# Half of three weight quarters requested from ScalarE's DMA queue instead of SyncE's

## The chip, the cores and the metric

The kernel runs on one core of a Trainium2 chip. A core has five engines, each with its own instruction stream: TensorE (PE, matrix multiply, with weight loads shown apart as PEld), VectorE (DVE), ScalarE (ACT), GpSimd (POOL) and SyncE (SP, which here only requests DMA transfers). ACT can request transfers too; a request stands in ACT's instruction stream between its computing instructions. Sixteen DMA engines carry out the transfers of all requesters. The metric is the device time of one execution in microseconds (us).

## What is computed

Inputs are q, k, v and an output gate of shape (4, 8, 768, 40) (batch, heads, time, head size), an input and a forget gate of shape (4, 8, 768), and two weight matrices, w_in (320 x 2048) and w_out (2048 x 320). The first block is an mLSTM cell, a recurrence over time for each batch and head, cut here to its core:

```python
m_new = np.maximum(f[t] + m, i[t])
f_stab, i_stab = np.exp(f[t] + m - m_new), np.exp(i[t] - m_new)
C = f_stab * C + i_stab * outer(v[t], k[t])
n = f_stab * n + i_stab * k[t]
y[t] = sigmoid(o[t]) * (C @ q[t]) / max(abs(n @ q[t]), 1)
```

Its output is reshaped to x of shape (3072, 320), 40 columns for each head, and goes through a feed-forward layer: `h = x @ w_in`, `g = max(0.01 * h, h)`, `out = g @ w_out`. The two weight matrices arrive as float64, since they are products of a float32 array and a float64 scalar; everything else is float32.

## The kernel before

**Work and its stages.** Time is cut into 6 chunks of 128 positions, and each chunk of each of the 4 batches is a step, s = 4 * chunk + batch, 24 in all. A step computes the cell for 8 heads in parallel form (scores, masks of decay, a carried state). The four steps of a chunk together make a group of 512 tokens for the feed-forward layer. The first chunk, steps 0 to 3, is written out by hand in `first_chunk` (L1184): it loads k, q, v and o of each step (`load_first`), does the scores and values, transposes the gated result into xT (`u_x`, copies on ACT, L861 and L862), and starts the first feed-forward units of group 0 (`ffs[0]`, `ffs[1]`). A unit of group 0 (`half`, in `ff_units`) is 20 matmuls of a 64-row slice of w_in against half of the group's tokens (L872), and an activation on ACT (L880, the leaky relu) that frees the two PSUM banks. From L1319 on a loop works through the feed-forward units of one group, with the cell's steps of the next chunk placed between them; from group 1 on with other products (L929, L1036).

**Weights.** w_in is taken in four quarters of 512 columns, n = 0 to 3 (`load_weights`, L238). A quarter's raw 64-bit words land in a buffer of 128 partitions: the lower 64 partitions hold 5 blocks of 64 rows for columns 0 to 255 of the quarter, and the upper 64 partitions the 5 blocks for columns 256 to 511 in another order (`SLOTS`, L74), so that the lower half (r = 0) is one request of 640 KB and the upper half (r = 1) two, of 512 and 128 KB. Quarters 1 to 3 (`WHOLE`) are loaded so; quarter 0 comes in two parts. Raw words of quarter 1 lie in `acts`, those of 2 and 3 in `raw`. `narrow_weights` (L280) then turns a half quarter into float32: two activations on ACT (L302, L303) and four instructions on DVE (L304 to L311). w_out follows in eight parts, narrowed in the same way.

**Order.** PE, DVE, ACT and POOL run their instructions in the order in which the program writes them (`manual_schedule`, L1281). SP's requests made through `Ordered` (L89) keep the program's order too. Where requests of different queues stand among each other is planned when the program is built, as is which semaphore counts a request's completion: eight of them are handed out in turn to the requests of both queues, and a request first waits until the transfer that last used its semaphore has landed.

Around the change, SP asks in this order: quarter 1 (three requests, 24.90 to 27.52 us), the gate values a of chunk 1, written to DRAM (L360), q of step 4, quarter 2 (28.99 to 31.59), k and v of step 4, the decay masks w of step 4 (from a in DRAM, spread over partitions), the output gate of step 4, quarter 3 (43.39 to 46.22), the output gate of step 5, k of step 5, a part of w_out, the masks of step 5, and so on. ACT asks for nothing between 4.8 and 156 us. Its stream at this place is: `prep_o(2)` and `prep_o(3)`, the tanh of the output gates (L583); the relu of `ffs[1]` (L880); the copies of xT for steps 2 and 3 (L861, L862), which the feed-forward unit that starts at 38.49 reads; the narrowing of quarter 1 (L302 at 38.16); then, in the loop, that of quarters 2 and 3 (from 43.65 and 58.52). On PE, `u_split` (L638) transposes k and q of step 4 at 45.33, and `u_parts` (L725, L731) reads step 5's scaled k (`vu`, made on POOL at L567 behind the masks, L537) at 69.41.

Of the kernel before, what the change touches and what calls it, by code (L numbers as in the profile page):

```python
# [18 lines left out]
def kernel(  # L19
# [26 lines left out]
    nc = tc.nc  # L46
# [54 lines left out]
    sync, by_act = queues = Ordered(nc.sync), Ordered(nc.scalar)  # L101
# [20 lines left out]
    for u in range(2):  # L122
        part = ident[ts(u, SL), ts(u, SL)]
        nc.gpsimd.affine_select(
            part, part, compare_op=ALU.not_equal, fill=1.0, base=0, pattern=[[-1, SL]], channel_multiplier=1,
# [80 lines left out]
    def run_of(r, at):  # L206

        ks = SLOTS[r][at:]
        return ks[0], next((i for i in range(1, len(ks)) if ks[i] != ks[i - 1] + 1), len(ks))
# [25 lines left out]

    WHOLE = (1, 2, 3)

    def load_weights(n, es=(0, 1)):  # L238

        m = n - QN  # L240
        if n < QN:
            dst = w_in[:, n, :]
        else:
            dst = w_out[:, 2 * m : 2 * m + 2, :].rearrange("p a d -> p (a d)")
        to = dst
        if wide:
            if n < 2:
                at = NF * GT - 2 * WC * (n + 1)
                raw = acts_l[:, at : at + 2 * WC].bitcast(U64)
            elif n < QN:  # L250
                raw = raw_t[:, WC * (n - 2) : WC * (n - 1)]
            elif m < 2:
                raw = w_out[:].rearrange("p f d -> p (f d)")[:, (2 + m) * WC : (3 + m) * WC].bitcast(U64)
            else:
                at = (4, 0, 1, 2, 3, 4)[m - 2] * HW
                raw = raw_t[:, at : at + HW]
            raws[n] = (raw, dst)
            to = raw
        if n < QN:
            src = moe_w_in[:, n * QC : (n + 1) * QC].rearrange("(k p) (r c) -> r p k c", p=DP, r=2)  # L260
            halves = to.rearrange("p (e k c) -> p e k c", e=2, k=KC)
            both = to.rearrange("p (k c) -> p k c", k=KC)
            if n in WHOLE:
                es = es[:1] if es[0] == 0 else ()
            for e in es:
                for r in range(2):
                    at = 0
                    while at < KC:
                        k0, n_k = run_of(r, at)
                        if n in WHOLE:  # L270
                            rows, part = both[DP * r : DP * (r + 1), at : at + n_k], src[r, :, k0 : k0 + n_k, :]
                        else:
                            rows, part = halves[DP * r : DP * (r + 1), e, at : at + n_k], src[r, :, k0 : k0 + n_k, ts(e, P)]
                        sync.dma_start(rows, part)
                        at += n_k
        else:
            rows = moe_w_out[2 * m * P : 2 * (m + 1) * P, :]
            sync.dma_start(to.rearrange("p (a d) -> p a d", d=Dm), rows.rearrange("(a p) d -> p a d", p=P))
# [41 lines left out]
    def gates(c):  # L320


        m0 = m0s.get(c)
        n = BH
        fc, il = (f0[:BH], i0[:BH]) if c == 0 else (fi[c][:, 0, :], fi[c][:, 1, :])
        F = wk.tile([n, P], F32, name="F", bufs=1)
        nc.vector.tensor_tensor_scan(F[:], fc, zeros[:n].to_broadcast([n, P]), 0.0, op0=ALU.add, op1=ALU.add)
        if c > 0:
            nc.vector.tensor_scalar(il, il, scalar1=m0[:], scalar2=None, op0=ALU.subtract)
        m = wk.tile([n, P], F32, name="m", bufs=1)  # L330
        nc.vector.tensor_tensor_scan(m[:], fc, il, -1e30 if c == 0 else 0.0, op0=ALU.add, op1=ALU.max)
        a = wk.tile([n, P], F32, name="a", bufs=1)
        nc.vector.tensor_tensor(a[:], F[:], m[:], op=ALU.subtract)
        bu = wk.tile([n, 3, P], F32, name="bu", bufs=1)
        nc.vector.tensor_tensor(bu[:, 0, :], il, F[:], op=ALU.subtract)
        if c + 1 < NB:
            m1 = wk.tile([BH, 1], F32, name="m0")
            if c == 0:
                nc.vector.tensor_copy(m1[:], m[:, P - 1 :])
            else:  # L340
                nc.vector.tensor_tensor(m1[:], m0[:], m[:, P - 1 :], op=ALU.add)
            m0s[c + 1] = m1
        if c > 0:
            na = wk.tile([BH, 1], F32, name="na")
            nc.vector.tensor_tensor(na[:], m[:, SL - 1 : SL], F[:, SL - 1 : SL], op=ALU.subtract)
        bus[c] = bu, a, (na if c > 0 else None)
# [71 lines left out]
    def load_first(s, i):  # L418

        d = st.setdefault(s, {})  # L420
        at = 4 * HW * 2 + s * Dm
        dst = (kn[:, s, :, :D], qn[:, s, :, :D], S_t[s][:, 1, :, :D], blocks(raw_l[:, at : at + Dm]))[i]
        d["k"], d["q"], d["va"], d["o"] = kn[:, s], qn[:, s], S_t[s][:, 1], raw_l[:, at : at + Dm]
        sync.dma_start(dst, (k, q, v, o_gate)[i][s, :, :P, :].rearrange("h p d -> p h d"))

    def natural(s, i):

        t = rb_t[s % NR][:, i]
        return t[:, : H * D].rearrange("p (h d) -> p h d", d=D)
# [26 lines left out]
    def raw_blocks(s, i, w):  # L456

        return blocks(rb_t[s % NR][:, i, QW : QW + RL])[:, :, :w]
# [121 lines left out]
    def prep_o(s):  # L580

        o = st[s]["o"] if s < B else natural(s, 2) if s < 2 * B else raw_blocks(s, 2, DB)
        nc.scalar.activation(o, o, AF.Tanh, scale=0.5)  # L583
# [169 lines left out]
    def u_values(s):  # L753
        d = st[s]
        pool, tag = (psc, "c") if s < 2 else (psf, "mm")
        pa = d["pa"] = pool.tile([P, H, D1], F32, name="pa", tag=tag)
        for h in range(H):
            for u in range(2):
                toks = ts(u, SL)
                nc.tensor.matmul(pa[toks, h, :], lhsT=d["w"][:, h, toks], rhs=d["va"][:, h, :D1], start=True, stop=True)  # L760
# [354 lines left out]
    def u_gates(c):  # L1115
        gates_T(c, bus.pop(c)[0])
# [67 lines left out]
    def first_chunk():  # L1184

        for n in range(2):
            for i in range(3):
                load_first(n, i)
        for n in range(2):
            load_first(n, 3)  # L1190
        load_weights(0, (0,))
        on_v, on_s = nc.vector.tensor_copy, nc.scalar.copy
        gates(0)
        gates_exp(0)
        load_fi(2)
        idle(3)
        ab = spread_masks()
        bu, a, _ = bus[0]
        a, left = replicate(a, bu)
        u_transpose(0, (on_v, on_v))  # L1200
        gates(1)
        spread_first(ab, a, left, 0)
        gates_T(0, bu)
        prep_vu(0)
        first_exps(ab, 0)
        u_scores(0)
        u_transpose(1, (on_s, on_s))
        prep_vu(1)
        prepare_tiles()
        u_values(0)  # L1210
        u_scores(1)
        ab = spread_masks()
        spread_first(ab, a, None, 2)
        e = next_exps(ab, 2)
        w, w1 = narrow_weights(0, 0), narrow_weights(0, 1)
        n0, n1 = narrow_weights(1, 0), narrow_weights(1, 1)
        prep_o(0)
        prep_o(1)
        gate(0)
        u_values(1)  # L1220
        load_first(2, 0)
        load_first(2, 1)
        load_weights(0, (1,))
        load_first(3, 0)
        load_first(3, 1)
        load_first(2, 2)
        load_first(3, 2)
        load_first(2, 3)
        load_first(3, 3)
        load_weights(1, (0,))  # L1230
        load_weights(1, (1,))
        run(e, 6)
        state(0)
        state(1)
        run(w, 2)
        u_x(0)
        gate(1)
        run(w, 4)
        u_x(1)
        state_copy(0)  # L1240
        state_copy(1)
        prepare_step(0)
        prepare_step(1)
        run(e, 2)
        ffs = ff_units(0)
        u_transpose(2, (on_s, on_s))
        run(e, 4)
        gates_exp(1)
        run(w1, 2)
        run(e, 4)  # L1250
        ffs[0]()
        run(w1, 2)
        prep_vu(2)
        prep_vu(3)
        u_scores(2)
        u_transpose(3, (on_v, on_s))
        run(w1, 2)
        u_gates(1)
        u_scores(3)
        prep_o(2)  # L1260
        prep_o(3)
        u_values(2)
        ffs[1]()
        gate(2)
        u_values(3)
        gate(3)
        u_x(2)
        state(2)
        u_x(3)
        state(3)  # L1270
        state_copy(2)
        run(n0, 4)
        state_copy(3)
        run(n0, 2)
        run(n1, 6)
        prepare_step(2)
        prepare_step(3)
        return ffs
# [160 lines left out]
```

## Time and profile before

| | |
|---|---|
| time, median of 3 runs | 473.57 us (472.79, 473.57, 474.94) |
| profiled execution: its own time | 473.84 us |
| profiled execution: its span, first to last instruction | 472.0 us |
| TensorE clock granted | 1.00 |
| SP's queue (q1) | 120944 packets, 51.15 MB |
| ACT's queue (q10) | 39984 packets, 7.17 MB |

How to read it: a profile line of the order in time has start (us), length, engine, line of the kernel, operation, what it writes <- what it reads, shape, count, and in brackets the idle time before it with what ended that. "SPq" and "ACTq" are DMA requests in the two engines' streams; their length is the time for which they hold the stream, which includes waiting for room. In the table by stage each row has the stage, its length, then for PE, PEld, DVE, ACT and POOL the busy time with the number of instructions, then the granted clock, the DMA engines' mean busy share and GB/s. "Landed" is the time of the last increment of a transfer's semaphore in the trace's records. A list of waits has: who <- what ended the wait: us in total, how many, the longest.

### The profile page before, as it was taken

Reading aid. Unit: us, or ns where it says so; the run is one execution under the profiler, and the core shown is the slowest. Engines: PE = TensorE matmul, PEld = TensorE weight load, DVE = VectorE, ACT = ScalarE, POOL = GpSimd, SP = SyncE. Lnnn points to the kernel's source line nnn. Section 1 sums busy time; section 2 is a strip of 40 time slices with the busy share of each in tenths; the row PEclk is TensorE's granted clock in tenths of the full one; section 3 lists DMA queues with packets and bytes.
Section 4 is the critical chain, followed back from the end, with each engine's and each line's share of the span. In section 5 each row is a group of like instructions: output and inputs, shape, how many; then the busy total and the mean of one; then the engine's idle time right before and its main releaser. Section 6 shows DMA issues by size and latency. Waiting matters only on the chain.

```text
span 472.0 us, 14167 instructions
## 1 busy us (share of the span) xinstructions
PE 463.1 (98%) x5716; PEld 416.3 (88%) x5716; DVE 336.8 (71%) x609; ACT 203.4 (43%) x497; POOL 171.7 (36%) x225
## 2 busy tenths in 40 slices
PE   9899999999999999999999999999999999999997
PEld 6677978777788999988999988999988999988997
DVE  5778688999479988867788867788847786104541
ACT  2657878755336511366311366311456311253210
POOL 4332377264335164923214923214822005300020
PEclk9999999999999999999999999999999999999999
DMA  9999998887732695865754865853875202100001
GB/s 130 169 192 187 188 205 220 206 181 145 153 110 65 159 166 112 176 153 129 171 119 106 181 130 126 198 114 79 188 151 124 74 9 81 58 0 2 8 8 42
DMA packets 160993, 59.21 MB, mean 125 GB/s; under 512 B 123808, under 2 KB 152352, under 8 KB 160928
## 3 DMA queue, kind: packets, MB, share of 16 engines
q1 hardware_dynamic: 120944, 51.15, 48.9%
q10 hardware_dynamic: 39984, 7.17, 9.4%
q8 instruction: 45, 0.74, 0.7%
q14 instruction: 20, 0.16, 0.1%
HBM read 51.58 MB, written 6.70 MB: 123 GB/s over the span
## 4 chain that ended last, share of the span: by engine, by line
PE 87%; SPq 5%; POOL 3%; issue 3%; DVE 1%; DMA 1%; ACT 0%; POOLq 0%
PE ph L1036 33%; PE po L929 33%; PE po L894 8%; SPq L95 5%; PE pT L813 3%; PE ph L872 3%; PE sd L725 3%; PE sd L731 1%; DMA raw<-in_o_gate_dram 1%; PE hN L785 1%; POOL w L537 1%; POOL y L576 1%; POOL S L701 1%; PE pa L760 0%; PE tk L638 0%
## 5 line engine op out<-in xcount | busy, mean ns | idle before, releaser
L929 PE MATMUL po<-w_out,acts 128*128 128x160 f32 x640 | 89.1, 300 | 0.0
L929 PEld LDWEIGHTS po<-w_out,acts 128*128 128x128 f32 x640 | 87.3, 190 | 0.6 <-ACT acts L1061 0.3
L1036 PE MATMUL ph<-xT,w_in 64*128 64x256 f32 x720 | 82.7, 378 | 0.0
L1036 PEld LDWEIGHTS ph<-xT,w_in 64*128 64x128 f32 x720 | 69.2, 187 | 8.6 <-issue 0.6
L1065 DVE TENSOR_TENSOR acts<-acts,ph 128x512 f32<-128x512 f32 x60 | 38.4, 683 | 40.7 <-PE ph L1036 40.6
L929 PE MATMUL po<-raw,acts 128*128 128x160 f32 x480 | 66.4, 300 | 0.0
L929 PEld LDWEIGHTS po<-raw,acts 128*128 128x128 f32 x480 | 65.4, 190 | 0.3
L537 POOL TENSOR_SCALAR_AFFINE_SELECT w<-w 64x512 f32<-64x512 f32 x40 | 34.0, 850 | 52.9 <-DMA w<-a_dr 51.7
L1069 ACT COPY acts<-ph 128x512 f32<-128x512 f32 x60 | 32.2, 588 | 48.8 <-PE ph L1036 48.8
L1061 ACT ACTIVATE acts<-acts 128x1024 f32<-128x1024 f32 x30 | 31.6, 1055 | 41.8 <-DVE acts L1065 32.4
L701 POOL TENSOR_TENSOR S<-S,f 40x336 f32<-40x336 f32 x36 | 30.6, 849 | 47.8 <-PE pT L813 32.1
L547 ACT ACTIVATE w<-w,gT 128x64 f32<-128x64 f32 x160 | 41.6, 337 | 11.7 <-DMA a_dr<-a 4.3
L742 DVE TENSOR_TENSOR qn<-w,sd 64x384 f32<-64x384 f32 (+1 forms) x80 | 33.4, 418 | 14.3 <-ACT acts L1069 8.4
L872 PE MATMUL ph<-xT,w_in 64*128 64x256 f32 x320 | 37.3, 381 | 0.9 <-issue 0.7
L894 PE MATMUL po<-w_out,acts 128*128 128x320 f32 x128 | 36.7, 437 | 0.0
L1036 PE MATMUL ph<-acts,w 64*128 64x256 f32 x320 | 36.3, 379 | 0.0
L827 POOL TENSOR_TENSOR xb<-xb,den 128x320 f32<-128x320 f32 x16 | 11.6, 727 | 67.0 <-DVE xb L824 64.7
L872 PEld LDWEIGHTS ph<-xT,w_in 64*128 64x128 f32 x320 | 31.9, 187 | 3.8 <-ACT w_out L303 0.9
L1036 PEld LDWEIGHTS ph<-acts,w 64*128 64x128 f32 x320 | 30.6, 187 | 3.6
L894 PEld LDWEIGHTS po<-w_out,acts 128*128 128x128 f32 x128 | 23.5, 190 | 9.2 <-ACT acts L880 0.3
L967 POOL TENSOR_TENSOR y<-y,raw 128x160 f32<-128x160 f32 x10 | 9.5, 950 | 59.5 <-ACT y L966 59.5
L612 DVE TENSOR_TENSOR qn<-kqT,ea 64x512 f32<-64x512 f32 x32 | 30.0, 939 | 0.8
(184 smaller groups left out, 732.2 us busy)
## 6 DMA issues: line engine op xcount, KB each, us to landing
rb<-in_k_dram SPq DMA_DIRECT2D x64, 80.0 KB
rb<-in_q_dram SPq DMA_DIRECT2D x64, 80.0 KB
rb<-in_o_gate_dram SPq DMA_DIRECT2D x64, 80.0 KB
ea<-a_dr SPq DMA_DIRECT2D x32, 128.0 KB
raw<-in_moe_w_out_dram SPq DMA_DIRECT2D x6, 640.0 KB
w<-a_dr ACTq DMA_DIRECT2D x24, 128.0 KB
x_dr<-x SPq DMA_DIRECT2D x64, 40.0 KB
xT<-x_dr SPq DMA_DIRECT2D x16, 160.0 KB
```

What stands on the lines that cost most here:

```text
L537: nc.gpsimd.affine_select(part, part, compare_op=ALU.is_ge, fill=-1e30, base=0, pattern=[[0, H], [1, SL]], channel_multiplier=-1,)
L547: yield nc.scalar.activation(w[:, h, :], w[:, h, :], AF.Exp, bias=gT[c][:, 0, bh : bh + 1], scale=1.0)
L612: nc.vector.tensor_tensor(mixed(s)[rows, 1 - r], d["kqT"][rows, 1].rearrange("p (h t) -> p h t", t=SL), d["ea"][rows], op=ALU.mult,)
L701: nc.gpsimd.tensor_tensor(new, old, g, op=ALU.mult)
L742: nc.vector.tensor_tensor(mixed(s)[toks, u, hs], w[toks, hs], bank[1 - u][to[u][hs.start], hs], op=ALU.mult,)
L872: nc.tensor.matmul(ph[r][:, cols], lhsT=w_row(r, slot, j), rhs=xT[DP * r : DP * (r + 1), slot, cols], start=(slot == 0), stop=(slot == KC ...
L894: nc.tensor.matmul(po[n][:], lhsT=acts[:, f, ts(n, P)], rhs=w_out[:, f, :], start=(f == 0), stop=(f == NF - 1),)
L929: nc.tensor.matmul(bank[:], lhsT=left[:, f, :], rhs=right[:, f, :], start=f == 0, stop=f == KH - 1)
L1036: nc.tensor.matmul(bank[r][:, e, :], lhsT=left(r)[rows, e], rhs=right(r)[rows], start=first and e == 0 and m == 0, stop=e == 1 and m == le ...
L1061: nc.scalar.activation(to, z, AF.Prelu, alpha=0.01)
L1065: nc.vector.tensor_tensor(to[:, 2 * r : 2 * r + 2], to[:, 2 * r : 2 * r + 2], bank[r], op=ALU.add)
L1069: nc.scalar.copy(to[:, 2 * r : 2 * r + 2], bank[r])
```

## The change

The requests for the upper 64 partitions of quarters 1, 2 and 3 of w_in, two for each quarter, are taken out of SP's order and made by ACT, all six in a row, right behind the tanh of step 3. The lower halves stay where they were on SP. The bytes, the destinations and the number of requests are the same. For quarter 1 the request comes later in the program than before, for quarter 2 a little earlier, for quarter 3 much earlier.

```diff
-    def load_weights(n, es=(0, 1)):
+    def load_weights(n, es=(0, 1), rs=None):
...
             if n in WHOLE:
                 es = es[:1] if es[0] == 0 else ()
             for e in es:
-                for r in range(2):
+                for r in ((0,) if n in WHOLE else (0, 1)) if rs is None else rs:
                     at = 0
                     while at < KC:
...
-                        sync.dma_start(rows, part)
+                        (sync if rs is None else nc.scalar).dma_start(rows, part)
                         at += n_k
...
         prep_o(2)
         prep_o(3)
+        for n in WHOLE:
+            load_weights(n, rs=(1,))
         u_values(2)
         ffs[1]()
```

## The prediction

> **What bounds the kernel now.** I read the page first: busy times, slices, chain.
>
> ```profile
> PE 463.1 (98%) x5716; PEld 416.3 (88%) x5716; DVE 336.8 (71%) x609; ACT 203.4 (43%) x497; POOL 171.7 (36%) x225
> ...
> PE   9899999999999999999999999999999999999997
> ...
> DMA  9999998887732695865754865853875202100001
> ...
> PE 87%; SPq 5%; POOL 3%; issue 3%; DVE 1%; DMA 1%; ACT 0%; POOLq 0%
> ```
>
> TensorE (PE) is busy 463.1 of 472.0 us, so the kernel can lose far more than it can gain: all PE idle time is 9 us. The change lies in slices 3 to 5 (24 to 56 us), where the DMA engines are full. The table by stage says how much PE idles there:
>
> ```profile
> 24.00:30.00 6.00, 4.90 (x53) 4.17 (x51) 4.14 (x7) 5.44 (x18) 2.55 (x5) 1.00 1.05 184
> 30.00:36.00 6.00, 6.00 (x107) 5.10 (x104) 4.46 (x16) 0.90 (x3) 1.54 (x5) 1.00 1.14 200
> 36.00:44.00 8.00, 7.36 (x89) 6.67 (x90) 6.43 (x15) 5.64 (x13) 0.25 (x1) 1.00 1.15 186
> 44.00:56.00 12.00, 11.29 (x156) 10.66 (x153) 10.08 (x17) 10.12 (x28) 5.87 (x7) 1.00 1.01 168
> 56.00:70.00 14.00, 12.91 (x338) 10.66 (x339) 9.59 (x17) 11.12 (x28) 8.54 (x11) 1.00 0.90 217
> ```
>
> The first count is PE's busy time, the number before the last the DMA share (1.00 and above is full), the last GB/s. PE idles 3.5 us in 24 to 70; from 70 to 126 it idles not at all. Next, ScalarE (ACT) where the six new requests go, in order of time:
>
> ```profile
> 28.61 0.83 ACT L583 ACTIVATE raw<-raw 128x320 f32<-128x320 f32 x2
> 34.32 0.66 ACT L880 ACTIVATE acts<-ph 128x256 f32<-128x256 f32 x2 [4.88 <-PE ph L872]
> 35.76 0.37 ACT L861 COPY xT<-xt 128x256 f32<-128x256 f32 x1 [0.78 <-PE xt L860]
> 36.09 0.48 ACT L862 COPY xT<-xe 128x384 f32<-128x384 f32 x1
> 37.42 0.37 ACT L861 COPY xT<-xt 128x256 f32<-128x256 f32 x1 [0.86 <-PE xt L860]
> ```
>
> The two tanhs (L583) of steps 2 and 3 end at 29.44; then ACT is idle 4.88 us, and later 0.78 and 0.86. Then SyncE (SP) in order of time, and what its queue waited for between 28 and 37 us:
>
> ```profile
> 28.99 2.60 SPq L95 DMA_DIRECT2D raw<-in_moe_w_in_dram x3
> 31.88 1.32 SPq L95 DMA_DIRECT2D kn<-in_k_dram  x1
> 34.50 1.02 SPq L95 DMA_DIRECT2D acts<-in_v_dram  x1
> 36.10 6.61 SPq L95 DMA_DIRECT2D w<-a_dr  x2
> ```
>
> ```profile
> SPq L95 <- DMA acts<-in_moe_w_in_dram: 1.5, 2, 1.2
> ```
>
> The second is the line that matters. The load of k for step 4 (31.88) and of v (34.50) write nothing that w_in touches, yet waited for pieces of w_in to land. The semaphore records say why: all DMAs, of SP and of ACT alike, share eight completion semaphores in turn, and a DMA waits until the one eight before it has landed. k of step 4 is the eighth behind the first piece of quarter 1 (landed 31.82), v the eighth behind the second (34.42). Landing is slow here: pieces asked at 24.9 to 30.3 landed 6.9 to 12.5 us later.
>
> Last, PE where it uses all this:
>
> ```profile
> 38.49 6.91 PE L872 MATMUL ph<-xT,w_in 64*128 64x256 f32 x60
> 45.33 0.25 PE L638 MATMUL tk<-ident,kn 64*40 64x64 f32 x2
> ...
> 69.41 0.23 PE L731 MATMUL sd<-S,vu 64*40 64x42 f32 x1 [0.90 <-POOL vu L567]
> ```
>
> **The change, part by part.** Its sum goes against the profiled execution, 473.84 us (span 472.0 and 1.8 around it), which is 0.27 above the median 473.57.
>
> *Six issues leave SP* (two each at 26 to 27.5, 29.6 to 31.6, 44 to 46.2 us). They are worth nothing by themselves: SP waits on landings and the DMA engines are full from 0 to 56 us, so an earlier request only queues. If the engines had room, the gain would be the waits that DMA feeds: 0.90 at 69.41 and at most 0.7 "issue" at 46.8.
>
> *Six issues join ACT.* SP's pieces of the same shape take 0.60 to 0.63 us unhindered, so six are 3.8. At the start of the kernel a DMA of ACT was issued 0.01 us behind the start of the activation before it (3.87 against 3.86), so they begin about 29.0 and end at 32.8, before the relu at 34.32. The cover is 4.88 us of idle time. If it is gone: ACT then owes relu 0.66, copies 0.81 and 0.81 before PE can start the 60 matmuls of 38.49, and 0.78 + 0.86 of idle time can close up. Released at T, ACT ends these at T + 2.28, against 38.23 now: PE is late by T - 35.95.
>
> *Bytes change places.* Quarter 3's upper piece (640 KB) is asked for at about 32 instead of 44 to 46. Its two parts took 51.64 to 55.14, 3.5 us of full engines; whatever it passes lands 3.5 us later. Without another delay that is k of step 4, landed 43.67, which PE wants at 45.33: 1.66 spare, 1.8 late. Masks of step 4 (landed 45.8) have 5 us: GpSimd ended that chain (vu) at 51.25, PE takes it from 56.4. Quarter 1's upper piece is asked 2.5 us later than now (landed 35.44); its reader is ACT at 38.16, 2.7 spare.
>
> *The semaphores in turn*, the term that decides. Each of ACT's six waits for the DMA eight before it in the planned order, and ACT's relu and copies queue behind. Counted from what SP may have asked by then: quarter 1's lower piece, a, q of step 4, quarter 2's lower piece, k of step 4 (all free to go by about 28.5 once two pieces are gone from before them); then ACT's first three; then v of step 4, which is free when VectorE has narrowed quarter 0 (30.98); then ACT's last three. Eight before the fourth is a, before the fifth q, before the sixth quarter 2's lower piece. So ACT is held until that lands. It lands at 39.49 now. Quarter 1's upper piece, 3.62 us of it (31.82 to 35.44), is no longer in SP's line: 35.9 if nothing of ACT's passes it. If ACT's first five do, they add 3.62, 3.27 (quarter 2, 39.49 to 42.76) and 2.99 (quarter 3's larger part, 51.64 to 54.63): 45.7. The nearest row for who goes first: ACT's 16 KB asked at 3.87 landed at 7.21, before SP's 160 KB asked at 3.01 (8.48), but 3.3 us after it was asked, where an empty queue took 1.7. So ACT's packets pass part of SP's: I take the middle, 40.8, and with the last issue, 0.62, T = 41.4. PE is late by 5.45. Behind it the 0.90 wait at 69.41 is gone, since masks of step 5 (landed 59.7) keep their time: the bytes ahead of them are the same. Sum: 473.84 + 5.45 - 0.90 = 478.4; against the median, 478.1. Ends of the term: T = 36.5 makes +0.55, eaten by the 0.90; T = 46.4 makes +10.4 - 0.9 = 9.5, so 483.1.
>
> The Trainium skill, "DMA: Bandwidth & Descriptors", section "Rules for kernel authors", says not to bother with two transfers to disjoint partition halves, since both spread over the same 16 engines and serialize. By that alone the time would stay at 473.6; it speaks against a gain and agrees with the full DMA share above, but says nothing of a held ScalarE.
>
> **Rivals.**
> 1. *ACT is not held.* The planned order puts the six early enough that the DMAs eight before them have landed (up to the o gates of step 3, landed 28.84, and quarter 1's lower piece, 31.8). For it: six fit in the idle time; SP's real order at 29 us is only just past k of step 4. Then only k of step 4 is late, 1.8 us at 45.33, of which 0.90 comes back at 69.41: 474.5 (473.2 to 475.9). This is not slower by what can be measured. It decides if ACT is released before 35.95.
> 2. *ACT is held longer.* Its 2 KB packets alternate one for one with SP's, whose q of step 4 has 160-byte packets, so all of ACT's five go first: the upper end, 483.1 (480.5 to 484.5). The same comes if the six are planned behind v of step 4, waiting for k (43.67 now). Against it: the 7.21 landing above.
> The Trainium skill, "DMA: Bandwidth & Descriptors", section "Queues, rings and completion order", states such taking of turns, packet by packet, between the queues of one DMA engine; the row of 7.21 agrees in part.
> 3. *SP's relief pays.* v, masks and k of step 5 come earlier because SP's line is shorter, and the 0.90, 0.7 and 0.33 of PE waits at 69.4, 46.8 and 45.0 go: 473.57 - 1.9 = 471.6. Against it: engines full, same bytes. It needs ACT free before 35.95 and a faster drain with two queues; over 0.5% it would need more idle time than is there.
>
> **How the numbers follow.** Likeliest, ACT held: 0.50, at 478.1, own range 475.5 to 481. Rival 1: 0.29. Rival 2: 0.14. Rival 3: 0.07, of which 0.04 above 0.5%. What a measurement can tell from no change is about 0.5%, 2.4 us: the three runs before spread 472.79 to 474.94. Of the held case 0.03 falls within that, so slower 0.61, same 0.35, faster 0.04. The range leaves out rival 3's lower half and the slowest of rival 2: 473.0 to 483.0.
>
> **What would show it.** Right: six ACT queue issues behind L583, the last of them late, at 36 to 46 us; the 4.88 idle before the relu grown and put down to a DMA; the 60 matmuls starting 2 to 8 us after 38.49; the 0.90 before 69.41 gone; from 126 us on all as before, shifted. Wrong: six issues in one row at 29 to 33 us and the relu at 34.3; then PE waits before tk at 45.33 if rival 1 holds, and nowhere if rival 3 does. The prediction fails first at the planned order, which the trace of before can't show, and next at who goes first among the two queues.

## The result, and the profile after

The change made the kernel slower by 2.5%: 485.88 us median (484.76 to 486.71, four runs) against 474.25 us (472.79 to 476.03, four runs) of the kernel before; the ratio is 1.0252, 95% interval 1.0221 to 1.0283. An execution more than 1.5% above the fastest of its kernel counts as slow and enters no ratio below; that is one, of 479.24 us, in the last experiment. The profiled execution took 485.48 us, its span is 483.7 us. The forecast was 478.1 us, with 483.0 as its upper end: right in direction and place, too small by 7.8 us.

The page of the kernel after, busy times, PE's slices and clock, and the chain:

```profile
PE 464.4 (96%) x5716; PEld 416.1 (86%) x5716; DVE 335.7 (69%) x609; ACT 203.2 (42%) x497; POOL 171.3 (35%) x225
...
PE   9892899999999999999999999999999999999997
...
PEclk9997799999999999999999999999999999999999
...
PE 87%; ACT 3%; DVE 3%; DMA 3%; SPq 2%; issue 1%; POOL 0%; ACTq 0%; DVEq 0%; POOLq 0%
```

PE does the same 5716 matmuls, but the fourth slice (36.3 to 48.4 us) fell from 9 to 2, and the granted clock is 7 tenths in the fourth and fifth, where it was full before. Everything else looks as it did. The same stages as before, kernel after:

```profile
30.00:36.00 6.00, 6.00 (x104) 5.20 (x103) 4.85 (x13) 0.35 (x1) 1.02 (x3) 1.00 1.13 200
36.00:44.00 8.00, 2.84 (x52) 2.10 (x48) 2.25 (x8) 0.00 (x0) 0.77 (x2) 0.96 1.14 197
44.00:56.00 12.00, 5.37 (x36) 4.57 (x38) 4.06 (x8) 5.42 (x12) 4.41 (x7) 0.60 1.13 201
56.00:70.00 14.00, 13.92 (x229) 12.05 (x231) 9.37 (x18) 11.60 (x33) 3.90 (x4) 1.00 0.91 206
```

PE idles 11.8 us in 36 to 56, where it idled 1.4 before. The DMA engines are as full as they were (1.13 to 1.14) and move slightly more, 197 to 201 GB/s: the bytes aren't what is missing. ACT computes nothing at all from 36 to 44. ACT in order of time says why:

```profile
28.74 0.69 ACTq L274 DMA_DIRECT2D acts<-in_moe_w_in_dram  x1
32.31 0.53 ACTq L274 DMA_DIRECT2D acts<-in_moe_w_in_dram  x1
36.07 12.76 ACTq L274 DMA_DIRECT2D raw<-in_moe_w_in_dram  x4
48.87 0.78 ACT L880 ACTIVATE acts<-ph 128x256 f32<-128x256 f32 x2 [18.52 <-DMA rb<-in_o_gate_dram]
```

The six requests took from 28.74 to 48.83 us to be made, and the relu, 34.32 before, stood behind them until 48.87. Its idle time, 4.88 us before and ended by PE, is now 18.52 us and is ended by a transfer with which the relu has nothing to do, the output gate of step 4. The semaphore records give the order that was planned across both queues. The columns are: place in that order, who asked, when the request was made, when it landed.

```
place  by   asked   landed  what                          eight places before it
 31    SP   27.66   36.05   quarter 2, lower
 32    SP   28.36   42.01   k of step 4
 33    ACT  28.74   39.99   quarter 1, upper (512 KB)     v of step 3, 27.1
 34    SP   31.97   43.82   v of step 4
 35    SP   32.43   45.39   masks of step 4
 36    SP   36.95   47.13   masks of step 4
 37    ACT  32.31   41.07   quarter 1, upper (128 KB)     a, landed 32.29
 38    SP   38.72   48.32   output gate of step 4
 39    ACT  36.07   46.61   quarter 2, upper (512 KB)     quarter 2, lower, 36.05
 40    SP   42.03   52.10   quarter 3, lower
 41    ACT  40.01   48.93   quarter 2, upper (128 KB)     ACT's own first, 39.99
 42    ACT  43.84   54.34   quarter 3, upper (512 KB)     v of step 4, 43.82
 46    ACT  48.34   55.42   quarter 3, upper (128 KB)     output gate of step 4, 48.32
```

Five of the six requests are made 0.02 to 0.03 us after the request eight places before them has landed. The last one waits for the output gate of step 4, which SP itself could only ask for at 38.72. PE in order of time shows what that did:

```profile
50.63 8.16 PE L872 MATMUL ph<-xT,w_in 64*128 64x256 f32 x60 [10.67 <-ACT xT L861]
58.72 0.25 PE L638 MATMUL tk<-ident,kn 64*40 64x64 f32 x2
...
69.70 0.24 PE L731 MATMUL sd<-S,vu 64*40 64x42 f32 x4
...
94.29 1.34 PE L894 MATMUL po<-w_out,acts 128*128 128x320 f32 x4 [0.25 <-DVE w_out L311]
```

The 60 matmuls start 12.14 us later than at 38.49, behind one wait of 10.67 us for ACT's copies, and take 8.16 us instead of 6.91. Step 4's transposes of k wait for nothing, and the wait before the products with `vu` is gone. The 1.25 us that the 60 matmuls grew by are put down to the clock; in the profiles of other versions that ran them at full clock they took 6.75 to 7.38 us, so its price is 0.8 to 1.4 us. Windows of the kernel after around the wait, the granted clock being the number after POOL's:

```profile
39.00:43.00 4.00, 0.30 (x4) 0.11 (x1) 0.00 (x0) 0.00 (x0) 0.00 (x0) 1.00 1.14 193
43.00:44.00 1.00, 0.00 (x0) 0.00 (x0) 0.00 (x0) 0.00 (x0) 0.00 (x0) 0.65 1.05 218
44.00:50.00 6.00, 0.00 (x0) 0.00 (x0) 0.00 (x0) 1.12 (x4) 4.12 (x7) 0.50 1.11 212
50.00:53.00 3.00, 2.37 (x12) 1.94 (x14) 1.28 (x3) 3.00 (x7) 0.29 (x1) 0.50 1.35 163
53.00:54.00 1.00, 1.00 (x10) 0.86 (x8) 0.96 (x3) 0.64 (x1) 0.00 (x0) 0.73 1.03 138
```

PE stopped at 39.95. A mean of 0.65 in 43 to 44 puts the halving at 43.30, 3.35 us later; 0.73 in 53 to 54 puts its end at 53.54, 2.9 us after PE had resumed. So the first matmuls behind the wait ran at half clock.

The kernel before had one more wait of PE behind the transposes, which is gone too:

```profile
47.55 8.90 PE L872 MATMUL ph<-xT,w_in 64*128 64x256 f32 x79 [0.71 <-issue]
```

Against the execution of before (473.84 us): start of the 60 matmuls +12.14, clock +1.25, the 0.90 us wait for `vu` and the 0.71 us of "issue" ahead of the next unit gone, a new 0.25 us wait for w_out. That makes 485.87, where 485.48 was measured.

### The profile page after: what moved, and what is told of

It is laid out like the page before. It is cut to its first block, busy times and chain, and to the rows that moved or that the text cites. A ratio compares the mean times of both kernels' runs of the same rounds, so it can differ in the third digit from the quotient of the medians.

```text
span 483.7 us, 14162 instructions
## 1 busy us (share of the span) xinstructions
PE 464.4 (96%) x5716; PEld 416.1 (86%) x5716; DVE 335.7 (69%) x609; ACT 203.2 (42%) x497; POOL 171.3 (35%) x225
## 4 chain that ended last, share of the span: by engine, by line
PE 87%; ACT 3%; DVE 3%; DMA 3%; SPq 2%; issue 1%; POOL 0%; ACTq 0%; DVEq 0%; POOLq 0%
PE ph L1036 33%; PE po L929 32%; PE po L894 7%; PE pT L813 3%; PE ph L872 3%; PE sd L725 3%; SPq L95 2%; DMA rb<-in_o_gate_dram 2%; ACT kqT L644 1%; PE sd L731 1%; PE ab L508 1%; PE hN L785 1%; PE tkq L652 1%; DMA w<-a_dr 1%; PE ab L492 1%
## 5 line engine op out<-in xcount | busy, mean ns | idle before, releaser
L1036 PE MATMUL ph<-xT,w_in 64*128 64x256 f32 x720 | 82.7, 378 | 0.0
L1065 DVE TENSOR_TENSOR acts<-acts,ph 128x512 f32<-128x512 f32 x60 | 38.4, 683 | 40.7 <-PE ph L1036 40.6
L872 PE MATMUL ph<-xT,w_in 64*128 64x256 f32 x320 | 38.7, 392 | 11.3 <-ACT xT L861 10.7
L1036 PE MATMUL ph<-acts,w 64*128 64x256 f32 x320 | 36.3, 379 | 0.0
```

The source lines that it names most:

```text
L872: nc.tensor.matmul(ph[r][:, cols], lhsT=w_row(r, slot, j), rhs=xT[DP * r : DP * (r + 1), slot, cols], start=(slot == 0), stop=(slot == KC ...
L1036: nc.tensor.matmul(bank[r][:, e, :], lhsT=left(r)[rows, e], rhs=right(r)[rows], start=first and e == 0 and m == 0, stop=e == 1 and m == le ...
L1065: nc.vector.tensor_tensor(to[:, 2 * r : 2 * r + 2], to[:, 2 * r : 2 * r + 2], bank[r], op=ALU.add)
```

## The experiments

The theory was that ACT is held by the completion semaphores, and that nothing else costs much. The rivals were the bytes (quarters 2 and 3 moved forward, others delayed) and two queues as such. Each ratio below is against runs of the kernel before on the same chip. A diff is against the kernel before where that is said, else against the kernel after.

**Requests of 2 KB.** Against the kernel before: all of w_in stays with SP, and six small requests that fill an unused buffer are put where the change put its six.

```diff
+    spare = consts.tile([P, 24], U64, name="spare")
...
         prep_o(3)
+        for n in range(6):
+            nc.scalar.dma_start(spare[DP:, 4 * n : 4 * n + 4], moe_w_in[n % KC * DP : n % KC * DP + DP, :4])
```

> The kernel before, with all of w_in asked for by SyncE as before, and six more requests of 2 KB each (64 partitions x 32 bytes, into a tile that nothing reads) on ScalarE behind the tanh of step 3. Theory (ScalarE is held by the eight completion semaphores in turn): in the planned order the sixth stands eight behind k of step 4, which landed at 43.7 us before; ScalarE is released at about 44, PE's 60 matmuls start about 8 us later than 38.5, and the time is 480 to 483 us, though no weight has changed its place. Rival (the weights' bytes on a second queue crowd out what SyncE asked for): 12 KB crowd out nothing, 473 to 475 us.

Measured: 484.00 us (481.48 to 484.36), ratio 1.0174 (1.0132 to 1.0216). ACT and PE in order of time (lines are one higher in this kernel):

```profile
35.05 10.75 ACTq L1264 DMA_DIRECT2D spare<-in_moe_w_in_dram  x6
45.85 0.75 ACT L881 ACTIVATE acts<-ph 128x256 f32<-128x256 f32 x2 [16.25 <-DMA spare<-in_moe_w_in_dram]
```

```profile
46.38 0.79 PE L682 MATMUL dC<-vu,kn 128*40 128x42 f32 x16 [8.88 <-ACT acts L881]
47.57 9.38 PE L873 MATMUL ph<-xT,w_in 64*128 64x256 f32 x60 [0.41 <-ACT xT L862]
```

Six requests that move next to nothing hold ACT until 45.80, where the change held it until 48.83: they are made at 35.05, 35.83, 36.36, 40.90, 43.95 and 45.32, each 0.02 to 0.1 us behind a landing (35.03, 35.81, 36.26, 40.88, 43.93, 45.30) of the request eight places before. Waiting without bytes makes 1.7 of the 2.5%. The time is above the 480 to 483 us expected: ACT was released at 45.8 instead of 44, and 2.47 us of half clock hadn't been counted. The 60 matmuls start 9.08 us late and take 9.38 us instead of 6.91, with the clock halved from 39.27 to 52.93; less the 0.90 and 0.71, and with a 0.27 us wait for w_out, that makes 484.05, where the profiled execution took 484.12.

**The same six by SP.** The edit replaces the engine, so the order of the program and the moved bytes stay, and ACT asks for nothing.

```diff
-                        (sync if rs is None else nc.scalar).dma_start(rows, part)
+                        sync.dma_start(rows, part)
```

> The changed kernel, but its six requests for the upper partitions are made by SyncE at the same place in the program (before q of step 4), none by ScalarE. Theory (hold): ScalarE has nothing to wait for; the bytes of quarter 3's upper piece still pass k of step 4, which lands about 3.5 us later, 47.2 us, so PE waits about 1.9 us at 45.3 and gets 0.9 back at 69.4: 473.5 to 476 us. Rival (the bytes' new place costs, on whatever queue): as slow as the changed kernel, 482 to 486 us.

Measured: 475.64 us (474.54 to 477.65), ratio 1.0019 (0.9999 to 1.0038). PE in order of time has one new wait, for k of step 4, which landed at 47.40 instead of 43.67:

```profile
47.44 0.25 PE L638 MATMUL tk<-ident,kn 64*40 64x64 f32 x2 [1.89 <-DMA kn<-in_k_dram]
```

So bytes in another order cost 0.2%, with an interval from nothing to 0.4%, and the rest of the loss needs ACT.

**The six by ACT, early in the planned order.** ACT's requests go through the same helper that keeps SP's in the program's order (`by_act`, the helper on ACT), which makes the plan place them as they are written.

```diff
-                        (sync if rs is None else nc.scalar).dma_start(rows, part)
+                        (sync if rs is None else by_act).dma_start(rows, part)
```

> The changed kernel, all six requests on ScalarE at the same place, but put into the written order of requests (behind quarter 1's lower piece, ahead of q of step 4), so that those eight before them are loads of steps 2 and 3 that landed by 28.2 us. Theory (hold): six ScalarE issues in a row end by about 33 to 34, ScalarE is not held, and only the later k of step 4 costs: 473.5 to 476.5 us. Rival (two queues compete for the DMA engines, so that SyncE's loads land late): 480 to 486 us.

Measured: 475.56 us (473.80 to 477.43), ratio 1.0023 (1.0003 to 1.0044). ACT, then PE, in order of time:

```profile
30.23 2.65 ACTq L95 DMA_DIRECT2D raw<-in_moe_w_in_dram  x4
35.49 0.66 ACT L880 ACTIVATE acts<-ph 128x256 f32<-128x256 f32 x2 [5.04 <-PE ph L872]
```

```profile
47.91 0.25 PE L638 MATMUL tk<-ident,kn 64*40 64x64 f32 x2 [1.36 <-DMA kn<-in_k_dram]
```

The same engine asks for the same bytes at the same point of its program; only the requests' places among those of SP differ. All six are made from 28.84 to 32.88, the relu waits for PE again and not for a transfer, and 10.3 of the 11.6 us between the medians of the kernels after and before are gone. This shows the cause: the places in the planned order, through the semaphores that come with them. What is left is the wait for k of step 4.

**Quarter 3 alone.** Two requests by ACT, placed by the plan as in the change; quarters 1 and 2 with SP.

```diff
-                for r in ((0,) if n in WHOLE else (0, 1)) if rs is None else rs:
+                for r in ((0,) if n == 3 else (0, 1)) if rs is None else rs:
...
-        for n in WHOLE:
+        for n in (3,):
```

> The changed kernel with quarters 1 and 2 back on SyncE, both halves; only quarter 3's two upper requests are on ScalarE behind the tanh of step 3. Theory (hold): its second request stands eight behind quarter 2's lower piece, landed 39.5 us before; ScalarE is released at about 40, PE is late by 4.2 us and gets 0.9 back: 476 to 478.5 us. Rival (bytes): a third of the changed kernel's 12 us, all of it by k of step 4 landing 3.5 us late: 474 to 476 us, with ScalarE free by 34.

Measured: 478.55 us (477.70 to 479.82), ratio 1.0078 (1.0047 to 1.0108). The second request was made at 40.13, behind quarter 2's lower piece (landed 40.11). ACT, PE and a window:

```profile
34.63 6.00 ACTq L274 DMA_DIRECT2D raw<-in_moe_w_in_dram  x2
40.69 0.66 ACT L880 ACTIVATE acts<-ph 128x256 f32<-128x256 f32 x2 [10.52 <-DMA raw<-in_moe_w_in_dram]
```

```profile
41.21 0.79 PE L681 MATMUL dC<-vu,kn 128*40 128x42 f32 x16 [3.16 <-ACT acts L880]
42.32 9.46 PE L872 MATMUL ph<-xT,w_in 64*128 64x256 f32 x60 [0.32 <-ACT xT L861]
```

```profile
41.00:47.00 6.00, 5.47 (x38) 4.48 (x40) 3.40 (x7) 4.36 (x11) 0.00 (x0) 0.50 1.18 194
```

Here ACT is released at about the time that the prediction had taken for the whole change, T = 40.7. The matmuls start 3.83 us late, take 2.55 us more at half clock (9.46 against 6.91), the 0.90 and 0.71 are gone, and the 0.26 us wait for w_out is there as in the change: 473.84 + 3.83 + 2.55 - 1.61 + 0.26 = 478.87, where the profiled execution took 478.61. A stall of 3.2 us cost some 2.6 more through the clock, which hadn't been expected; the delay that had been, 4.2, was about right.

**Quarter 1 alone.** As before, with `n == 1` and `(1,)`.

> The change for quarter 1 alone: its two upper pieces on ScalarE behind the tanh of step 3, quarters 2 and 3 with SyncE as before. By the planned order the second of the two has quarter 2's lower piece eight before it. Theory (hold): ScalarE is held until that lands, at 36 to 39.5 us as the other runs and the kernel before show for that piece, so T = 36.5 to 40.1 and PE is 0.5 to 4.1 late, 0 to 0.9 of it given back at 69 us, and little or no time at half clock: 474.4 to 478. ScalarE's second request is issued within 0.1 us of that landing. Rival (what costs is the bytes of quarters moved forward, and these are small here): 473.5 to 474.8 with the second request issued at once behind the first, before 32 us.

Measured: 482.58 us (481.69 to 483.51), ratio 1.0165 (1.0131 to 1.0198), well above both. The hold was as the theory had it (second request at 39.08, behind quarter 2's lower piece, landed 39.06), but the time was not. ACT, then PE:

```profile
28.92 10.66 ACTq L274 DMA_DIRECT2D acts<-in_moe_w_in_dram  x2
39.63 0.66 ACT L880 ACTIVATE acts<-ph 128x256 f32<-128x256 f32 x2 [10.24 <-PE xe L860]
...
46.01 0.78 ACT L302 ACTIVATE w_in<-acts 128x640 f32<-128x640 f32 x1 [4.41 <-DMA acts<-in_moe_w_in_dram]
```

```profile
41.26 2.85 PE L872 MATMUL ph<-xT,w_in 64*128 64x256 f32 x22 [0.60 <-ACT xT L861]
49.28 6.24 PE L872 MATMUL ph<-xT,w_in 64*128 64x256 f32 x38 [5.16 <-DVE S L689]
```

The request that is held is itself wanted soon. It landed at 45.90, and narrowing quarter 1 (L302) waited for it. The 5.16 us of PE are put down to DVE's last older work; PE was waiting for the narrowed quarter. Step 4's transposes come at 55.44 instead of 45.33: 2.77 us are the later start, 5.16 this wait, and 2.18 the longer time of the 60 matmuls (2.85 + 6.24 against 6.91), with the clock halved from 49.30 to 52.71. The expectation of little or no time at half clock failed as well. In the change this wait is hidden under the longer hold.

**Quarters 1 and 2, not held.** Through `by_act`, with `n in (1, 2)`; quarter 3 with SP at its old place.

> Upper pieces of quarters 1 and 2 asked for by ScalarE behind its tanh of step 3, but early in the written order, so that the requests eight before them have long landed and ScalarE isn't held; quarter 3 stays with SyncE at its old place. Theory: what was left as a cost in the run with all three quarters so placed was quarter 3's upper piece passing k of step 4 (1.36 us of PE's wait before tk). With quarter 3 back at its place that wait is under 0.3 us, k of step 4 lands at 43.7 to 45, and the time is the kernel before's within 0.3%: 473.2 to 475.5. Rival (relief of SyncE pays): 472 to 473, PE's waits at 45 to 47 and 69 us gone. Rival (two queues cost by themselves): 475.5 to 477.

Measured: 478.15 us (475.54 to 482.11), ratio 1.0078 (1.0048 to 1.0108): none of the three expectations, and a wide spread. ACT, then PE:

```profile
41.86 0.77 ACT L302 ACTIVATE w_in<-acts 128x640 f32<-128x640 f32 x1 [4.91 <-DMA acts<-in_moe_w_in_dram]
```

```profile
36.80 2.85 PE L872 MATMUL ph<-xT,w_in 64*128 64x256 f32 x22
44.55 6.93 PE L872 MATMUL ph<-xT,w_in 64*128 64x256 f32 x38 [4.89 <-DVE S L689]
```

ACT wasn't held, but its tanh waited for an output gate, so its first request came at 29.48 instead of 28.84. By then SP had asked for q of step 4 and, 0.01 us earlier, for quarter 2's lower piece. The 60 matmuls took 2.85 + 6.93 us instead of 6.91, with the clock halved from 42.54 to 49.37. These transfers landed in the order in which they had been asked for, whatever the queue:

```
asked    by   landed   what                   (quarters 1 and 2 by ACT)
28.80    SP   35.39    q of step 4
29.47    SP   39.09    quarter 2, lower
29.48    ACT  41.05    quarter 1, upper (512 KB)
30.20    ACT  41.76    quarter 1, upper (128 KB)
31.07    ACT  44.32    quarter 2, upper (512 KB)
31.72    ACT  45.12    quarter 2, upper (128 KB)
32.65    SP   45.72    k of step 4
33.13    SP   46.26    v of step 4
```

With all six by ACT, quarter 1's upper piece was asked for at 28.84 and SP's q of step 4 at 31.91; there the piece landed at 34.48 and q at 43.17. So the two profiles suggest that where ACT's pieces land depends on which of the two engines comes first, by tenths of a microsecond. That may be why the times spread over 6.6 us; it isn't shown. Half clock has a part in it: none of the twelve executions ran without (mean granted clock 0.989 to 0.996).

**Quarter 2 alone, not held.** Through `by_act`, with `n == 2` and `(2,)`.

> Quarter 2's upper piece alone by ScalarE, early in the written order, so that the requests eight before it have landed; quarters 1 and 3 with SyncE at their old places. The run with quarters 1 and 2 so placed lost 4.9 us because quarter 1's upper piece (asked at 29.5 by ScalarE) landed at 41.1 and 41.8, behind SyncE's q of step 4 and quarter 2's lower piece. Theory (the two queues are served about in the order of asking): quarter 1's upper piece is again in at 35 to 36, quarter 2's at 42 to 44, k of step 4 at 43.5 to 44.5, PE has no wait above 1 us between 30 and 69 us, and the time is 473.3 to 475.3 (ratio 0.998 to 1.002). Rival (a queue of ScalarE's beside SyncE's is slow by itself): quarter 2's upper piece lands at 46 or later, and the time is 476 to 479.

Measured: 473.67 us (471.64 to 475.98), ratio 0.9981 (0.9959 to 1.0002). ACT in order of time:

```profile
28.38 1.36 ACTq L95 DMA_DIRECT2D raw<-in_moe_w_in_dram  x2
35.55 0.66 ACT L880 ACTIVATE acts<-ph 128x256 f32<-128x256 f32 x2 [6.70 <-PE ph L872]
```

Quarter 1's upper piece, back with SP, was in by 35.06, k of step 4 by 43.69, and PE had no wait above 0.5 us between 30 and 69 us. The relu comes later than before, 35.55 against 34.32, and still waits for PE; PE ran at half clock here, from 28.66 to 35.49, without any stall to explain it:

```profile
29.00:35.00 6.00, 6.00 (x54) 5.01 (x52) 3.47 (x11) 0.00 (x0) 1.02 (x3) 0.50 1.11 204
```

The point on landing in the order of asking held roughly: ACT's larger piece, asked for 0.01 us ahead of q of step 4, landed at 39.07 ahead of q's 40.08; its smaller piece passed one of SP's that was asked for 0.23 us earlier. The forecast of 42 to 44 for ACT's piece was wrong, since it was asked for before that of SP.

**A busy PE during the hold.** The kernel after with 44, then 36 added matmuls of 128x512 bf16 (work that nobody reads) behind `state_copy(2)`, so that PE isn't idle while ACT is held.

```diff
         state_copy(2)
+        idle(44)
```

> The kernel after, with 44 matmuls of 128x512 bf16 whose result nobody reads, put on PE behind the last work it has before it waits for ScalarE (about 40 us), so that PE isn't idle while ScalarE is held; they add work and change nothing else. Theory: besides the 12.9 us that PE starts late, the halved clock at 43.3 to 53.4 us costs the 60 matmuls behind the wait 8.16 - 6.91 = 1.25 us. Then the granted clock stays at 0.98 or above through 40 to 56 us, the 60 matmuls take 6.9 to 7.0, ScalarE's relu is at 48.9 as in the kernel after, and the time is 1.0 to 1.5 us below that kernel's 485.9: 484.4 to 484.9. Rival: the clock costs nothing, since the work behind the wait is bound by the transposes' copies on ScalarE: 485.9 as there. If the dummies end later than ScalarE's release, the time is longer than 485.9 by what they run over.

> As the run with 44 added matmuls, with 36, since the 44 ended at 51.1, about 1.4 us behind the copies that PE waited for, their first 3.4 us being at half clock. Here they should end at 48.6 to 49.6, ahead of those copies, with the clock at full by then. Theory (clock): the 60 matmuls behind the wait take 6.7 to 6.9 at full clock, and the time behind ScalarE's release (time of the execution less the start of the relu; 485.48 - 48.87 = 436.6 in the kernel after) is 434.4 to 435.4. Rival (the clock costs nothing, for the copies bind): 436.3 to 436.9. The median is 484 to 485 by the first and 485.9 by the second.

Measured: 485.29 us (484.65 to 487.24) with 44, ratio 1.0229 (1.0193 to 1.0264), and 487.12 (486.49 to 487.62) with 36, ratio 1.0260 (1.0242 to 1.0278). PE with 44, then with 36:

```profile
39.60 0.23 PE L681 MATMUL dC<-vu,kn 128*40 128x42 f32 x1 [1.17 <-issue]
39.76 11.36 PE L370 MATMUL warm<-acts 128*128 128x512 bf16 x44
51.05 6.75 PE L872 MATMUL ph<-xT,w_in 64*128 64x256 f32 x60
```

```profile
39.27 7.94 PE L370 MATMUL warm<-acts 128*128 128x512 bf16 x36
50.57 8.43 PE L872 MATMUL ph<-xT,w_in 64*128 64x256 f32 x60 [3.36 <-ACT xT L861]
```

With 44 the clock was full when the 60 matmuls came, and they took 6.75 us: 1.41 less than in the kernel after. But the clock had halved at 39.96, as the added matmuls began, and they ended about 1.3 us too late (PE resumed 3.08 us behind the relu's start, 1.76 in the kernel after). The two cancel, so the total doesn't show the gain. One of the four executions shows a mean granted clock of 1.000; it took 484.86 us, which lies within the spread of the kernel after. With 36 they kept full clock and ended at 47.21; the 3.36 us of idle time left were enough to halve the clock from 51.38, after PE had resumed, and the 60 took 8.43, where 6.7 to 6.9 had been expected; the time fits neither expectation. Its profiled execution took 1.7 us more than that of the kernel after, and most of this is not the clock's: a 1.63 us pause of PE marked "issue" turned up at 92.8, whose cause stays open. The price of the clock is seen in the rows, some 1.3 to 1.7 us, and is not shown by a shorter time.

**Masks and v of step 5 ahead of w_out.** Against the kernel before; it goes after the 0.90 us wait at 69.41, and then also together with quarter 2 by ACT.

```diff
-        load_weights(QN + 0)
         feed(5, (2,))
         load_late(5, 1)
         feed(5, (1,))
+        load_weights(QN + 0)
```

> The kernel before, nothing on ScalarE; only the masks and v of step 5 are asked for ahead of the first part of w_out instead of behind it. Theory: the 0.90 us PE wait at 69.41 is for masks and v that came behind w_out's bytes; they now land about 3 us earlier, the wait goes, nothing waits for w_out before 81 us: 472.6 to 473.9 against 474.4, ratio 0.997 to 0.999. Rival: another wait takes its place (vu waits for VectorE, or the first matmuls with w_out at 81.5 wait): 474.0 to 475.

> The two edits that gave the shortest times so far, together: quarter 2's upper piece by ScalarE early in the written order, and masks and v of step 5 asked for ahead of the first part of w_out. Each took the 0.90 us wait at 69 us away by itself, so they don't add: one theory is that the time is that of either alone, 473.0 to 474.0 against 474.4, ratio 0.997 to 0.999, with an interval that may still touch 1. Rival: the gain of either was chance, ratio 0.999 to 1.001.

Measured: 473.85 us (472.28 to 478.27), ratio 0.9993 (0.9966 to 1.0020) alone, and 474.84 (471.28 to 479.24), ratio 1.0002 (0.9974 to 1.0030) together. The wait at 69.41 is gone from the profile of the first, and the time can't be told from no change. No version shown here beats the kernel before.

## Why the prediction was wrong in size

*ACT held by the eight semaphores, the term that decides.* The mechanism was right, named ahead with its place (six queue issues behind L583, the last one late, relu put down to a DMA). The step that failed is the order "k of step 4 ... then ACT's first three; then v of step 4 ...; then ACT's last three. Eight before the fourth is a, before the fifth q, before the sixth quarter 2's lower piece." In the planned order v, the two masks and the output gate of step 4 and quarter 3's lower piece stand among ACT's six, and three more of SP's ahead of the last. Quarter 2's lower piece is eight before the third; before the sixth it is the output gate of step 4. T was taken as 41.4, "the middle" of 36.5 and 46.4; it was 48.87, above the upper end. The middle, too, had stood on that wrong piece: it landed at 36.05, near the low end. So PE started 12.14 us late where 5.45 was forecast, which is 6.7 us of the miss.

*The formula* "PE is late by T - 35.95" gives 12.92 for T = 48.87, and PE started 12.14 late: the copies and PE closed up 0.8 us more than reckoned. Less the 0.90, the formula gives 485.9 from the right T; that this meets the median is luck, since the 0.8 too much and the 0.71 us of "issue" left out stand against the clock's 1.25 and the new wait of 0.25.

*The clock* is a term that the sum lacked: +1.25 here, and 2.18 to 2.87 in the four other runs without added matmuls in which PE stood still for 3.16 us or more. The 0.71 us of "issue" that went as well made up for a little over half of it.

*The 0.90 us at 69.41* went, as forecast, with the 0.71.

*Six issues in ACT's idle time* (3.8 us, hidden) was right where nothing holds them: 28.84 to 32.88, before a relu that waited for PE. *Six issues leaving SP, worth nothing* was right: no kernel with them off SP is faster beyond its interval.

*k of step 4 late by 1.8 us* was about right in size where ACT isn't held (PE waits 1.89 us by SP, 1.36 by ACT). In the change the hold covers it.

*Quarter 1's upper piece with "2.7 spare"* counted only the later asking. With quarters 1 and 2 by ACT, what SP had asked for in between landed ahead of it, and it was in at 41.76 instead of 35.44; with quarter 1 alone the hold put its second request off to 39.08, and it was in at 45.90. That cost PE 4.89 and 5.16 us. With all six early, asked for ahead of q of step 4, it was in at 35.17.

*Rivals.* The first, ACT not held, 474.5, is what the six early in the planned order give: 474.82 in the profiled execution, 475.56 in the median. The second named the case that came for five of the six, requests planned behind v of step 4, but as waiting for k and with 484.5 as its end. The third, SP's relief, fell; of its waits, the 0.33 at 45.0 was idle time of the weight loads, while PE computed until 45.40.

The Trainium skill, "DMA: Bandwidth & Descriptors", section "Rules for kernel authors", was quoted for two transfers to partition halves that serialize on the same engines. The same section says of spreading transfers over requesters that it only saves time on the sequencer. The run with the six early agrees, with a ratio of 1.0023: the bytes gained nothing by the second queue.

## What to carry to other kernels

Before a transfer is moved to a computing engine's queue, find out what its request will wait for: with eight completion semaphores handed out in turn, as here, it waits for the transfer eight places before it, of whatever queue, and the engine's later computing waits behind it. Look at the order as built rather than as written, and tie the requests to an early place if they go there at all. And count a stall of TensorE of 3 us or more as longer than it is: in all six profiles with such a stall (3.16 to 10.67 us) the 60 matmuls that it delayed ran in part at half clock and took 1.25 to 2.87 us more than the 6.91 of before.

## What was not expected of the hardware

The granted clock was halved for 10.24 us in the kernel after (43.30 to 53.54), for 13.65 with the requests of 2 KB (39.27 to 52.93), for 6.8 with quarter 3 alone (41.0 to 47.86), and for 3.42 and 3.40 with 44 and 36 added matmuls (39.96 to 43.38, 51.38 to 54.78), worked out from the means of one-microsecond windows: one to four times 3.4 us. It can come after the stall is over: with 36 added matmuls, PE resumed at 50.57 and the clock fell at 51.38. With 44, PE had idled only 1.17 and 0.46 us in the 3.4 us ahead of it. The Trainium skill, "TensorE: Matmul & The Clock Gate", section "Part 1: The HAM clock gate", tells of a window of about 3.4 us that runs freely and of half clock after an idle one. The lengths agree. By the case with 44, a window need not be wholly idle.

Half clock also came with no stall. With quarter 2 alone and with quarter 1 alone it lasted 6.83 us from 28.66 and from 28.82, before ACT's requests held anything, and PE had idled only 0.91 and 0.95 us in the 3.4 us ahead; the kernel before, with a wait of 0.99 us at the same place (28.25), kept full clock. What decides stays open. Half clock also goes with much of the spread: of the 74 executions of the kernel before that ran beside the experiments, 18 show a mean granted clock of 0.996 or less, with a median of 475.87 us, and 56 one of 0.999 or more, with 474.06. A ratio within 0.3% of 1 can be a matter of how many of them fall on either side.

Transfers of the two queues landed mostly in the order in which they had been asked for. The plainest case is a request of 2 KB: made by ACT at 35.05 with none of its own ahead, it landed at 44.53, among the pieces that SP had asked for before it. By the trace's packet records the first packet of ACT's queue started only at 41.63, 6.6 us after the request, and between the two that queue moved nothing. There are exceptions: in the kernel after, ACT's 128 KB asked for at 32.31 landed at 41.07, ahead of SP's k of step 4, asked for at 28.36 (42.01).
